# Bringing the slot weights to four groups of partitions with ScalarE copies in place of TensorE products

## The chip, the cores and the metric

The kernel runs on one core of one Trainium2 chip. The metric is the device time of one execution in microseconds (us); smaller is better. Three runs of the kernel before gave 720.49, 721.75 and 723.82 us, with a median of 721.75 us. Five engines work side by side, each in its own order and tied to the others by semaphores: TensorE (PE, with its weight loads as PEld), VectorE (DVE), ScalarE (ACT), GpSimd (POOL) and SyncE (SP), which issues the transfers.

## The reference, cut to what matters

The program is three layers, one behind the other, over 8 batches of 576 rows (4608 rows in all, 512 columns): a Nystrom attention, a gated feed-forward layer with 1536 hidden columns, and a soft mixture of 8 experts with 4 slots each, 32 slots in all. The change lies in the third:

```
logits = x @ phi                     # 4608 x 32
d = exp(logits - logits.max(0)); d /= d.sum(0)      # softmax down the rows, for each slot
slot_input = d.T @ x                 # 32 x 512
for e in range(8):                   # four slots for each expert
    slot_out[4*e:4*e+4] = relu(slot_input[4*e:4*e+4] @ w1[e]) @ w2[e]
c = exp(logits - logits.max(1)); c /= c.sum(1)      # softmax over the slots, for each row
out = c @ slot_out
```

The kernel never forms x. It keeps the hidden values h of the feed-forward layer (x = h @ w_out), sums `d.T @ h` batch by batch with a running maximum, and multiplies by w_out once at the end.

## The kernel before, in words

A batch is 48 places in the program: 12 blocks j of 128 hidden columns, with two halves of 288 rows each, with a gate product and a value product in each half. `unit` does one block. For each half `mm3` writes the gate product into a PSUM bank (`pg`, six matmuls), ScalarE makes `u` out of it (in the trace L299, the helper that records it, or L887, a tanh, in three of the 24 halves of batches 1 to 6, where DVE then finishes `u` at L888), `mm3` writes the value product into `pv`, and DVE multiplies the two into `hT` (L900 or L902). `logits` adds the block's share of the logits (`l`, L759), and `transposes` puts the hidden values into `HB` with rows on partitions (L764). The weights of the next two blocks come from `g_product` (`g`, L707) as a high part `GH` (ScalarE, L730) and a low part `GL` (DVE, L744).

All other work is laid between these places by tables (`SCHED`): the attention of the batch after, its row softmax, and, for the batch before, `softmoe`. A line of the table lists the places at which a generator runs on to its next `yield`; for `softmoe` that is `'sm': [1, 3, 5, 10, 17, 19, 20, 23, 24, 24, 27]`, so the step that the change touches is called at place 20 and the products that need it at place 23 of the batch that follows. The last batch has no batch behind it: its `softmoe` runs by itself after the last block, with `keep_warm` products (`warm`) between its steps. The Tile framework then places the instructions of each engine in an order of its own and sets the semaphores.

What `softmoe` does around the change: ScalarE raises the logits `LT` to their exponentials; DVE transposes them into `DN` (L820), 32 rows on each of the four groups of 32 partitions, `[128, 5 blocks, 32 slots]`. The sum over the rows of a batch is made of 32x32 tiles of TensorE: 18 row blocks times four column groups a, accumulated in four PSUM banks `m_d` (L844, 72 matmuls, shown as 144 in the trace since each is run in two parts). A tile reads its weights from its own group of 32 partitions, and row block g of `DN` lies on group g alone. So before the products every group of partitions must hold the weights of every row block. In the kernel before, `msum` (the 32x32 unit matrix repeated) times group g of `DN` gives a copy of that group on all 128 partitions: four products `m_dr` (L830), and four copies out of PSUM into `DR`, two by DVE and two by ScalarE (L833). `DR` lies in a spare part of the other batch's `HB`, so the trace calls it HB.

`m_dr`, `m_d` (three of its four banks), `g` and the attention's `m_a` and `m_c` all take turns in three PSUM banks with the tag `x`; the fourth bank of `m_d` is one of the two `pv` banks. After the products DVE adds them to the running sum `Sacc` (L852).

After the last batch come the products of the sum with w_out (`m_si`, L1107), the experts (`m_f`, L1153 and L1201), and the output (`m_o`, L1184). Their weights w1 and w2 are loaded ahead into buffers that come free on the way (`ffn_prefetch`, L962, and L970 in the end part).

Of the kernel before, what the change touches and what calls it, by code (L numbers as in the profile page):

```python
# [8 lines left out]
F32 = mybir.dt.float32  # L9
# [46 lines left out]
def nystrom_softmoe_kernel(  # L56
# [15 lines left out]
    pe, act, dve, pool, sp = nc.tensor, nc.scalar, nc.vector, nc.gpsimd, nc.sync  # L72
# [11 lines left out]
    psp = ctx.enter_context(tc.tile_pool(name="psp", bufs=1, space=PSUM))  # L84
# [7 lines left out]
    msum = cst[:, 256:384]  # L92
# [13 lines left out]
    DN = cp.tile([128, 5, M], F32, name="DN")  # L106
# [13 lines left out]
    spare = [HB[i][:, 6144:6912] for i in range(2)]  # L120
# [172 lines left out]
    def in_order(kind, *a, **kw):  # L293
        other = fence.get("exp" if kind == "silu" else "silu")
        if other is None:
            i = act.activation(*a, **kw)
        else:
            with tc.issue_after(other):
                i = act.activation(*a, **kw)  # L299
        fence[kind] = getattr(i, "ins", i)  # L300
# [467 lines left out]
    def keep_warm(n):  # L768

        m = psp.tile([128, 512], F32, tag="l", name="warm")  # L770
        for _ in range(n):
            pe.matmul(m[:, 0:160], ident, cst[:, 128:288], start=True, stop=True)
# [3 lines left out]
    def softmoe(b):  # L776
        L = L_t[b]
        assert ("l", b, NJ - 1) in seq
        act.copy(LT[:, 0:128], L[:, 0:128])
        act.copy(LT[0:64, 128:160], L[0:64, 128:160])  # L780

        pool.memset(LT[64:128, 128:160], -3e38)
        yield
        cm = smp.tile([128, 1], F32, tag="cm", name="cm")
        dve.tensor_reduce(cm, LT, axis=AX.X, op=ALU.max)
        c = CN[:, b]
        dve.transpose(c, LT.rearrange("p (k r) -> p k r", r=32))
        yield
        m = psp.tile([128, 512], F32, tag="x", name="m_x", bufs=3)
        pe.transpose(m[0:1, 0:128], cm[:, 0:1], ident)  # L790
        if b == nb - 1:
            keep_warm(WARM[0])
        row = smp.tile([1, 4, M], F32, tag="row", name="row")
        gm = smp.tile([1, M], F32, tag="gm", name="gm") if b else gmax
        dve.tensor_reduce(gm, m[0:1, 0:128].rearrange("p (c s) -> p s c", c=4), axis=AX.X, op=ALU.max)
        if b:
            dve.tensor_tensor(out=gmax, in0=gm, in1=gmax, op=ALU.max)
        dve.tensor_scalar(row, gmax.unsqueeze(1).to_broadcast([1, 4, M]), -1.0, None, ALU.mult)
        yield
        m = psp.tile([128, 512], F32, tag="x", name="m_y", bufs=3)  # L800
        pe.matmul(m[:, 0:1], row.rearrange("p c s -> p (c s)"), one, start=True, stop=True)
        mb = smp.tile([128, 2], F32, tag="mb", name="mb", bufs=2)
        dve.tensor_copy(mb[:, 0:1], m[:, 0:1])
        if b:
            dve.tensor_tensor(out=mb[:, 1:2], in0=mb[:, 0:1], in1=mb_t[-1][:, 0:1], op=ALU.subtract)
        mb_t.append(mb)
        mx = smp.tile([128, 5], F32, tag="mxc", name="mxc")
        bc = mx.unsqueeze(2).to_broadcast([128, 5, M])
        dve.tensor_reduce(mx, c, axis=AX.X, op=ALU.max)
        dve.tensor_tensor(out=c, in0=c, in1=bc, op=ALU.subtract)  # L810
        yield
        in_order("exp", LT, LT, AF.Exp, bias=mb[:, 0:1], accum_out=dsum)
        if b == nb - 1:
            keep_warm(WARM[1])
        al = smp.tile([128, 1], F32, tag="al", name="al")
        if b:
            in_order("exp", al, mb[:, 1:2], AF.Exp)
        in_order("exp", c, c, AF.Exp)
        yield
        dve.transpose(DN, LT.rearrange("p (k r) -> p k r", r=32))  # L820
        if b:
            dve.scalar_tensor_tensor(out=den, in0=den, scalar=al, in1=dsum, op0=ALU.mult, op1=ALU.add)
        else:
            dve.tensor_copy(den, dsum)
        yield

        DR = spare[(b + 1) % 2][:, 0:640].rearrange("p (g k s) -> p g k s", g=4, k=5)
        for g in range(4):
            m = psp.tile([128, 512], F32, tag="x", name="m_dr", bufs=3)
            pe.matmul(m[:, 0:160], msum[32 * g:32 * g + 32, :], DN[32 * g:32 * g + 32].rearrange("p k s -> p (k s)"),  # L830
                      start=True, stop=True)
            o = DR[:, g].rearrange("p k s -> p (k s)")
            act.copy(o, m[:, 0:160]) if g % 2 else dve.tensor_copy(o, m[:, 0:160])  # L833
        if b == nb - 1:
            keep_warm(WARM[2])
        yield

        assert ("h", b, NJ - 1) in seq
        ms = [psp.tile([128, 512], F32, tag="x" if a < 3 else "pv", name="m_d", bufs=3 if a < 3 else 2) for a in range(4)]
        hb = HB[b % 2].rearrange("p (j t f) -> p j t f", j=NJ, f=32)  # L840
        for k in range(5):
            for g in range(4 if k < 4 else 2):
                for a in range(4):
                    pe.matmul(ms[a][32 * g:32 * g + 32, 0:384].rearrange("p (j f) -> p j f", j=NJ),  # L844
                              DR[32 * a:32 * a + 32, g, k, :], hb[32 * a:32 * a + 32, :, 4 * k + g, :],
                              start=k == 0, stop=k == (4 if g < 2 else 3))
        if b == nb - 1:
            keep_warm(WARM[3])
        yield
        for a in (3, 0, 1, 2):  # L850
            if b:
                i = dve.scalar_tensor_tensor(out=Sacc[:, a], in0=Sacc[:, a], scalar=al, in1=ms[a][:, 0:384],  # L852
                                             op0=ALU.mult, op1=ALU.add)
                fence["sum"] = getattr(i, "ins", i)
            else:
                act.copy(Sacc[:, a], ms[a][:, 0:384])
            if a == 0:
                yield
        yield
        dve.tensor_reduce(mx, c, axis=AX.X, op=ALU.add)  # L860
        dve.tensor_scalar(mx, mx, 1e-9, None, ALU.add)
        dve.reciprocal(mx, mx)
        dve.tensor_tensor(out=c, in0=c, in1=bc, op=ALU.mult)
        yield
# [55 lines left out]
    for x in S_["loads"]:  # L920
        k, n = x[0], x[1:]
# [94 lines left out]
    for a in range(1, nb):  # L1016
        att, asm = attention(a), a_softmax(a)
        for gen, nm in ((att, "at"), (asm, "am")):
            for r in S_[nm + str(min(a, 3))]:
                todo[48 * (a - 1) + r].append(gen)  # L1020
        sm = softmoe(a - 1)
        for r in S_["sm"]:
            todo[48 * a + r].append(sm)
    prev = None
    for b in range(nb):
        for j in range(NJ):
            p = prev
# [40 lines left out]
    for _ in softmoe(nb - 1):  # L1068
        pass
# [11 lines left out]
    m = psp.tile([128, 512], F32, tag="x", name="m_s", bufs=3)  # L1081

    for a in (3, 0, 1, 2):
        for i in range(3):
            pe.matmul(m[:, 128 * i + 32 * a:128 * i + 32 * a + 32], Sacc[:, a, 128 * i:128 * i + 128], i4,
                      start=True, stop=True)
# [16 lines left out]
    m = psp.tile([128, 512], F32, tag="x", name="m_si", bufs=3)  # L1103
    for j in range(NJ):
        i, fb = divmod(j, 4)
# [5 lines left out]
    m = psp.tile([128, 512], F32, tag="x", name="m_sit", bufs=3)  # L1111
# [3 lines left out]
    for g in range(2):  # L1115
        for z, c in ((ZP3, slice(0, 3)), (ZP1, slice(3, 4))):
            for i in range(c.stop - c.start):
                o = z[:, i, 4 * g:4 * g + 4, 0:24].rearrange("p j (a x) -> p j a x", a=3)[:, :, :, 4 * g:4 * g + 4]
# [28 lines left out]
    for nh in range(2):  # L1147
        m = psp.tile([128, 512], F32, tag="pg", name="m_f1", bufs=2)
        for g in range(2):
            for c in range(4):  # L1150
                t = 8 * nh + 4 * g + c
                for e in range(4):
                    pe.matmul(m[32 * e:32 * e + 32, :], ZP[c][:, 4 * g + e, :], ffn_t[t][e],  # L1153
                              start=(g, c) == (0, 0), stop=(g, c) == (1, 3))
                pump(t + 1 + NT)
        act.activation(hF, m, AF.Relu)
        m = psp.tile([128, 512], F32, tag="x", name="m_ft", bufs=3)
        for i in range(4):
            pe.transpose(m[:, 128 * i:128 * i + 128], hF[:, 128 * i:128 * i + 128], ident)
        for g in range(2):  # L1160
            o = FT[:, g, 4 * nh:4 * nh + 4, :].rearrange("p i (x h s) -> p (i x) h s", h=2, s=4)[:, :, g, :]
# [32 lines left out]
    for dh in range(2):  # L1194
        m = psp.tile([128, 512], F32, tag="pg", name="m_f2", bufs=2)
# [72 lines left out]
```

## Time and profile before

| | |
|---|---|
| median of 3 runs | 721.75 us (720.49 to 723.82) |
| the profiled execution | 720.9 us, its span 719.1 us |
| TensorE matmul busy | 661.3 us (92%) |
| DVE busy | 510.8 us (71%) |
| ScalarE busy | 315.5 us (44%) |
| moved by the DMA queues | 105.04 MB, mean 146 GB/s |
| mean granted TensorE clock | 0.964 of full speed |

A busy share is a mean over the span. Where two engines take turns within a batch, a share says little about which of them ends last at a given place; that is read from the timeline and from the chain of work that ended last. Starts in the rows are us from the start of the span. In a row of the timeline, the number after the start is the time from the first start to the last end of the instructions that the row merges (`x2`, `x144`); what stands in brackets is the time for which the engine stood idle before it and the instruction that ended it.

### The profile page before, as it was taken

How to read it: one execution, taken by the hardware profiler on the slowest of the kernel's cores; microseconds unless marked ns; L12 is line 12 of the kernel's file. 1: busy time of each engine (PE TensorE's matmuls, PEld its weight loads, DVE VectorE, ACT ScalarE, POOL GpSimd, SP SyncE). 2: the span in 40 equal slices, each digit the busy share in tenths (PEclk: the TensorE clock that was granted, in tenths of full speed). 3: DMA queues.
4: the chain of work that ended last, by engine and by line, in shares of the span. 5: the costliest groups of instructions: out<-in, count | busy, mean ns of one | idle time of the engine just before them, and what ended most of it. 6: DMA issues, size and time to landing. Idle time of an engine off the chain costs nothing.

```text
span 719.1 us, 18723 instructions
## 1 busy us (share of the span) xinstructions
PE 661.3 (92%) x7755; PEld 488.0 (68%) x7755; DVE 510.8 (71%) x1222; ACT 315.5 (44%) x803; POOL 115.7 (16%) x132
## 2 busy tenths in 40 slices
PE   5787888999999999999999999999999999999980
PEld 2664566777687778767776877687778777773550
DVE  5999999877865896689578957885796664530441
ACT  2566766535533643264327333733363342311430
POOL 0544464401200120021012001200120000010000
PEclk9797898999999999999999999999999999999996
DMA  8687645304220431034012402240211399669999
GB/s 292 224 299 277 236 168 196 132 18 133 68 67 2 132 97 39 8 126 134 1 54 82 134 1 67 68 133 1 67 61 61 111 316 275 203 216 308 348 367 320
DMA packets 59989, 105.04 MB, mean 146 GB/s; under 512 B 3968, under 2 KB 29696, under 8 KB 58368
## 3 DMA queue, kind: packets, MB, share of 16 engines
q1 hardware_dynamic: 59904, 103.84, 44.1%
q8 instruction: 61, 1.00, 0.6%
q14 instruction: 24, 0.20, 0.1%
HBM read 91.24 MB, written 12.58 MB: 144 GB/s over the span
## 4 chain that ended last, share of the span: by engine, by line
PE 67%; DVE 17%; DMA 5%; ACT 5%; issue 3%; POOL 2%; SPq 0%; DVEq 0%; POOLq 0%; ACTq 0%
PE pg L873 20%; PE pv L873 17%; PE g L707 6%; PE l L759 5%; PE m_d L844 4%; PE m_n L634 3%; PE m_f L1153 2%; PE m_a L526 2%; DMA out_dram<-ob 1%; DVE w L179 1%; DMA HB<-in_w_dram 1%; DVE bd L309 1%; PE m_c L526 1%; DMA ffn<-in_w_dram 1%; DVE HB L179 1%
## 5 line engine op out<-in xcount | busy, mean ns | idle before, releaser
L299 ACT ACTIVATE u<-pg 128x288 f32<-128x288 f32 x174 | 71.5, 411 | 153.0 <-PE pg L873 146.3
L902 DVE TENSOR_TENSOR hT<-u,pv 128x288 f32<-128x288 f32 x162 | 72.9, 450 | 54.4 <-PE pv L873 47.6
L873 PE MATMUL pg<-EH,GH 128*128 128x288 f32 x384 | 98.2, 333 | 3.2 <-ACT GH L730 2.4
L873 PE MATMUL pv<-EH,GH 128*128 128x288 f32 x384 | 92.3, 314 | 0.8 <-DVE hT L902 0.8
L873 PE MATMUL pg<-EH,GL 128*128 128x288 f32 x384 | 87.1, 302 | 0.2 <-DVE GL L744 0.2
L744 DVE TENSOR_TENSOR GL<-g,GH 128x512 fp32r<-128x512 f32 (+1 forms) x114 | 63.2, 579 | 32.8 <-ACT GH L730 32.0
L873 PE MATMUL pg<-EL,GH 128*128 128x288 f32 x384 | 84.8, 302 | 0.0
L873 PE MATMUL pv<-EH,GL 128*128 128x288 f32 x384 | 84.6, 298 | 0.0
L873 PE MATMUL pv<-EL,GH 128*128 128x288 f32 x384 | 83.7, 299 | 0.0
L873 PEld LDWEIGHTS pg<-EH,GH 128*128 128x128 f32 x384 | 61.1, 192 | 25.0 <-issue 18.8
L764 DVE STREAM_TRANSPOSE HB<-hT 128x576 f32<-128x576 f32 x96 | 73.9, 770 | 1.6 <-POOL hT L898 0.2
L873 PEld LDWEIGHTS pv<-EH,GH 128*128 128x128 f32 x384 | 62.1, 190 | 18.4 <-issue 16.8
L730 ACT CAST GH<-g 128x512 fp32r<-128x512 f32 (+1 forms) x114 | 51.6, 505 | 51.0 <-PE g L707 50.8
L873 PEld LDWEIGHTS pg<-EH,GL 128*128 128x128 f32 x384 | 63.5, 191 | 2.5 <-issue 1.5
L873 PEld LDWEIGHTS pg<-EL,GH 128*128 128x128 f32 x384 | 62.6, 192 | 3.4 <-issue 3.4
L873 PEld LDWEIGHTS pv<-EH,GL 128*128 128x128 f32 x384 | 63.3, 191 | 0.0
L873 PEld LDWEIGHTS pv<-EL,GH 128*128 128x128 f32 x384 | 62.7, 191 | 0.0
L707 PE MATMUL g<-w,WB 64*32 64x512 f32 (+1 forms) x976 | 59.3, 511 | 1.6 <-DVE nx L621 0.7
L759 PE MATMUL l<-hT,P_sb 128*32 128x128 f32 (+1 forms) x768 | 48.5, 301 | 0.6 <-DVE hT L902 0.6
L759 PEld LDWEIGHTS l<-hT,P_sb 128*32 128x32 f32 x768 | 16.2, 109 | 40.0 <-issue 18.0
L680 POOL TENSOR_TENSOR AN<-AN,mxA 128x576 f32<-128x576 f32 x16 | 18.3, 1165 | 152.8 <-DVE mxA L679 136.9
L844 PE MATMUL m_d<-HB,HB 32*32 32x384 f32 x1152 | 40.7, 491 | 0.3 <-DVE GL L744 0.3
(252 smaller groups left out, 1057.5 us busy)
## 6 DMA issues: line engine op xcount, KB each, us to landing
k<-in_kT_dram SPq DMA_DIRECT2D x52, 288.0 KB, 3.9
ffn<-in_w_dram SPq DMA_DIRECT2D x13, 1024.0 KB, 9.2
ffn<-in_w_dram SPq DMA_DIRECT2D x24, 512.0 KB, 8.8
HB<-in_w_cat_dram SPq DMA_DIRECT2D x8, 1024.0 KB, 6.5
v<-in_v_dram SPq DMA_DIRECT2D x8, 1024.0 KB, 5.8
q<-in_qT_dram SPq DMA_DIRECT2D x28, 288.0 KB, 3.5
HB<-in_w_out_dram SPq DMA_DIRECT2D x12, 512.0 KB, 5.4
out_dram<-ob SPq DMA_DIRECT2D x5, 1024.0 KB, 10.4
```

The source lines that it names most:

```text
L299: i = act.activation(*a, **kw)
L526: pe.matmul(ms[r][32 * hp:32 * hp + 32, 0:HALF], lm[64 * r:64 * r + 64, hp, :], qk_t[nm, b, hp][64 * r:64 * r + 64, HALF * half:HALF * hal ...
L634: pe.matmul(m[:, 96 * q:96 * q + 96], bd[:, q, :], RV[:, q, :], start=True, stop=True)
L680: lambda q: pool.tensor_tensor(out=AN[q], in0=AN[q], in1=bc[q], op=ALU.subtract),
L707: pe.matmul(gs[r][32 * hp:32 * hp + 32, 0:256 * n].rearrange("p (u f) -> p u f", u=n), WB[b % 2][64 * r:64 * r + 64, hp, :], w[64 * r:64 * ...
L730: act.copy(H_, g)
L744: dve.tensor_tensor(out=GL, in0=g, in1=GH, op=ALU.subtract)
L759: pe.matmul(L[32 * c:32 * c + 32, 0:32 * k], P_sb[:, j, :], main[:, 0:k, c, :], start=j == 0, stop=j == NJ - 1)
L764: dve.transpose(HB[b % 2][:, S * j:S * j + S].rearrange("p (t r) -> p t r", r=32), hT[:, 0:S].rearrange("p (t r) -> p t r", r=32))
L844: pe.matmul(ms[a][32 * g:32 * g + 32, 0:384].rearrange("p (j f) -> p j f", j=NJ), DR[32 * a:32 * a + 32, g, k, :], hb[32 * a:32 * a + 32, ...
L873: pe.matmul(ps[:, 0:HALF], G_t[b, j, q, sel_][h], e[:, q, ts_], start=n == 0, stop=n == 5)
L902: dve.tensor_tensor(out=o, in0=u, in1=pv[:, 0:HALF], op=ALU.mult)
```

## The change

The four products and their four copies go. Group a of partitions needs row block g; with `DX[a ^ g]` in place of `DR[:, g]`, block g is read by group a from the tile of number a XOR g. `DX[0]` is `DN` itself. `DX[1]` is `DN` with groups 0 and 1 and groups 2 and 3 exchanged (four copies of 32 partitions), `DX[2]` is `DN` with the two halves of 64 partitions exchanged (two copies), and `DX[3]` is `DX[1]` with its halves exchanged (two copies, which must wait for `DX[1]`). All eight copies are 160 elements long on 32 or 64 partitions, read SBUF and write SBUF at other partitions, and are ScalarE's; in the last batch three of them are DVE's. The products `m_d` keep their number, shapes and order.

```diff
-        DR = spare[(b + 1) % 2][:, 0:640].rearrange("p (g k s) -> p g k s", g=4, k=5)
-        for g in range(4):
-            m = psp.tile([128, 512], F32, tag="x", name="m_dr", bufs=3)
-            pe.matmul(m[:, 0:160], msum[32 * g:32 * g + 32, :], DN[32 * g:32 * g + 32].rearrange("p k s -> p (k s)"),
-                      start=True, stop=True)
-            o = DR[:, g].rearrange("p k s -> p (k s)")
-            act.copy(o, m[:, 0:160]) if g % 2 else dve.tensor_copy(o, m[:, 0:160])
+
+        DX = [DN] + [spare[(b + 1) % 2][:, 160 * i:160 * i + 160].rearrange("p (k s) -> p k s", k=5) for i in range(3)]
+        for i, (x, src, to, fro, n) in enumerate(((2, 0, 0, 64, 64), (1, 0, 0, 32, 32), (1, 0, 32, 0, 32), (2, 0, 64, 0, 64),
+                                                  (1, 0, 64, 96, 32), (1, 0, 96, 64, 32), (3, 1, 0, 64, 64), (3, 1, 64, 0, 64))):
+            if b == nb - 1 and i in (0, 3, 7):
+                dve.tensor_copy(DX[x][to:to + n], DX[src][fro:fro + n])
+            else:
+                act.copy(DX[x][to:to + n], DX[src][fro:fro + n])
...
-                              DR[32 * a:32 * a + 32, g, k, :], hb[32 * a:32 * a + 32, :, 4 * k + g, :],
+                              DX[a ^ g][32 * a:32 * a + 32, k, :], hb[32 * a:32 * a + 32, :, 4 * k + g, :],
```

Where this stands on the engines: the orders below are those of ScalarE and TensorE in the blocks 4 and 5 of batch 3, where the weights of batch 2 are brought out, and of ScalarE after the last block. A line number of the changed kernel is larger by one from L830 on (L887 is L888 there, and so on).

ScalarE in batch 3, before: `CE` are the attention's scores, `u` the gate halves, `GH` the weights of the next two blocks.

```order
L557 COPY CE_3745<-m_c 128x320
L557 COPY CE_3746<-m_c 128x320
L887 ACTIVATE u<-pg 128x288
L833 COPY HB_86<-m_dr 128x160 x2
L299 ACTIVATE CE_3745,stat<-CE_3745,stat 128x576
L299 ACTIVATE CE_3745,stat<-CE_3745,stat 128x32
L299 ACTIVATE CE_3746,stat<-CE_3746,stat 128x576
L730 CAST GH<-g 128x512 x2
```

The same place in the changed kernel:

```order
L557 COPY CE_3737<-m_c 128x320
L557 COPY CE_3738<-m_c 128x320
L834 COPY HB_86<-DN 64x160
L834 COPY HB_86<-DN 32x160 x2
L834 COPY HB_86<-DN 64x160
L888 ACTIVATE u<-pg 128x288
L834 COPY HB_86<-DN 32x160 x2
L834 COPY HB_86<-HB_86 64x160 x2
L299 ACTIVATE CE_3737,stat<-CE_3737,stat 128x576
L299 ACTIVATE CE_3737,stat<-CE_3737,stat 128x32
L299 ACTIVATE CE_3738,stat<-CE_3738,stat 128x576
L730 CAST GH<-g 128x512 x2
```

Four copies now stand ahead of `u` and four behind it, in place of two behind it; the exponentials and `GH` keep their order behind them. Of the pair that reads HB, the first waits for ScalarE's own copies.

TensorE at the same place, before: two value products are parted by the last of the four `m_dr`.

```order
L873 MATMUL pg<-EH,GL 128x288 x2
L830 MATMUL m_dr<-DN,cst 128x160 x3
L873 MATMUL pv<-EH,GH 128x288
L830 MATMUL m_dr<-DN,cst 128x160
L873 MATMUL pv<-EH,GH 128x288
L873 MATMUL pv<-EL,GH 128x288 x2
L873 MATMUL pv<-EH,GL 128x288 x2
L707 MATMUL g<-w_602,WB_76 32x512 x8
```

In the changed kernel the four `m_dr` are gone and all else stands as it did, `m_d` too, one block later. On DVE the two copies L833 are gone, between L571 and L568 in batch 3, and nothing else moved.

ScalarE after the last block, before:

```order
L299 ACT_TABLE_LOAD
L299 ACTIVATE CN<-CN 128x160
L299 ACTIVATE LT,dsum<-LT,mb 128x160
L299 ACTIVATE al<-mb 128x1
L833 COPY HB_85<-m_dr 128x160 x2
L1133 CAST HB_86<-CN 128x20x8
```

And in the changed kernel:

```order
L299 ACT_TABLE_LOAD
L299 ACTIVATE CN<-CN 128x160
L299 ACTIVATE LT,dsum<-LT,mb 128x160
L299 ACTIVATE al<-mb 128x1
L834 COPY HB_85<-DN 32x160 x4
L834 COPY HB_85<-HB_85 64x160
L1134 CAST HB_86<-CN 128x20x8
```

Here ScalarE makes `DX[1]` and half of `DX[3]`; DVE makes `DX[2]` right behind `DN`, and, behind a reciprocal and a product (L862 and L863 of the kernel before), the other half of `DX[3]`. On TensorE the four `m_dr` between `warm` and `m_d` are gone.

## Rows read from the trace of the kernel before

**Rows 1.** The page's part 4: shares of the chain that ended last, by engine.

```profile
PE 67%; DVE 17%; DMA 5%; ACT 5%; issue 3%; POOL 2%; SPq 0%; DVEq 0%; POOLq 0%; ACTq 0%
```

**Rows 2.** Instructions on m_dr: count, ns min/median/max, first and last start, forms.

```profile
L830 PE MATMUL m_dr<-DN,cst x64: 294/346/399, 175.4 to 634.3; 32*128 32x160 f32 x64
```

**Rows 3.** The chain that ended last, in batch 3: start us, us, what.

```profile
317.78 0.53 DVE HB L833 x2
...
320.95 1.29 DVE GL L744 x2
```

**Rows 4.** Timeline of batch 3, 311.5 to 328 us: start, us, engine, instruction.

```profile
313.40 0.33 ACT L299 ACTIVATE CN<-CN 128x160 f32<-128x160 f32 x1
...
313.62 0.68 ACT L299 ACTIVATE AN<-AN 128x576 f32<-128x576 f32 x1
...
315.06 0.76 ACT L557 COPY CE<-m_c 128x320 f32<-128x320 f32 x2
...
315.62 0.43 PE L873 MATMUL pg<-EH,GL 128*128 128x288 f32 x2
...
316.09 0.41 ACT L887 ACTIVATE u<-pg 128x288 f32<-128x288 f32 x1 [0.27 <-PE pg L873]
...
317.28 0.45 DVE L888 SCALAR_TENSOR_TENSOR u<-u,pg 128x288 f32<-128x288 f32 x1
...
317.88 0.78 ACT L299 ACTIVATE CE<-CE,stat 128x576 f32<-128x576 f32 x1
...
318.26 1.09 PE L707 MATMUL g<-w,WB 64*32 64x512 f32 x16
...
319.58 0.78 ACT L299 ACTIVATE CE<-CE,stat 128x576 f32<-128x576 f32 x1 [0.53 <-DVE stat L571]
...
320.30 0.43 PE L873 MATMUL pg<-EH,GL 128*128 128x288 f32 x2
...
320.36 1.05 ACT L730 CAST GH<-g 128x512 fp32r<-128x512 f32 x2
...
321.45 5.14 PE L844 MATMUL m_d<-HB,HB 32*32 32x384 f32 x144
...
322.29 0.46 PEld L844 LDWEIGHTS m_d<-HB,HB 32*32 32x32 f32 x33 [0.46 <-DVE GL L744]
```

**Rows 5.** Timeline of batch 7, 586 to 602 us.

```profile
589.82 0.43 PE L873 MATMUL pg<-EH,GL 128*128 128x288 f32 x2
...
590.34 0.71 ACT L299 ACTIVATE u<-pg 128x288 f32<-128x288 f32 x2
...
592.61 0.66 PE L707 MATMUL g<-w,WB 64*32 64x256 f32 x16
...
593.36 0.65 ACT L730 CAST GH<-g 128x256 fp32r<-128x256 f32 x2 [1.21 <-PE g L707]
...
593.76 0.76 DVE L744 TENSOR_TENSOR GL<-g,GH 128x256 fp32r<-128x256 f32 x2 [0.53 <-ACT GH L730]
...
595.38 4.32 PE L844 MATMUL m_d<-HB,HB 32*32 32x384 f32 x144
```

**Rows 6.** Timeline after the last block, 625 to 645 us.

```profile
630.63 2.55 PE L772 MATMUL warm<-cst 128*128 128x160 f32 x12
...
631.01 0.43 ACT L299 ACTIVATE LT<-LT,mb 128x160 f32<-128x160 f32 x1 [1.11 <-DVE mb L803]
...
631.57 0.35 DVE L820 STREAM_TRANSPOSE DN<-LT 128x160 f32<-128x160 f32 x1
...
634.98 3.59 PEld L844 LDWEIGHTS m_d<-HB,HB 32*32 32x32 f32 x140 [0.31 <-ACT HB L833]
```

**Rows 7.** SP's waits, 640 to 719 us: engine line waited for: total, times, longest.

```profile
SPq L970 <- PE m_si L1107: 5.7, 2, 5.4
```

**Rows 8.** Busy time by stretch: per engine, then clock, DMA share, GB/s.

```profile
644.00:648.00 4.00, 4.00 (x96) 3.54 (x88) 0.01 (x1) 0.00 (x0) 0.00 (x0) 0.64 0.25 65
652.00:656.00 4.00, 4.00 (x42) 1.15 (x33) 0.00 (x0) 0.00 (x0) 0.00 (x0) 1.00 1.03 344
```

## The prediction, made before the changed kernel ran

> **What bounds the kernel now.** I read the chain of work that ended last first, since the busy shares lie near each other and do not say who waits. TensorE holds 67% of that chain and DVE 17% [rows 1], so both have stretches of their own, and the question at each of the eight places of the change is which of the two is late there. Then I read the rows of the instructions that go, then the timeline at the three kinds of place: batch 3 for the six alike ones (the weights brought out in batches 1 to 6), batch 7, and the end behind the last block.
>
> In batch 3 the four products `m_dr` stand in TensorE's way: from the last gate pair ahead of them to `g` it takes 318.26 - 315.62 = 2.64 us. The same pairs without `m_dr` (gate pair, three value pairs, change to the next kind) take 321.45 - 320.30 = 1.15 us a little later [rows 4]. So `m_dr` costs TensorE 1.49 us there, although the instructions of a batch are only some 0.35 us each in the list and overlap [rows 2]. But TensorE is not the one that is late: at 322.29 `m_d` has stood for 0.46 us until the second `GL` ends, because two of its banks are those of `g` [rows 4]. `GL` waits for `GH`, `GH` stands on ScalarE behind the exponential at 319.58, and that one waited 0.53 us for DVE's L571. The chain runs accordingly through DVE in this stretch, and the two copies L833 are a link of it with 0.53 us [rows 3].
>
> In batch 7 there is no such wait: `GL` ends at 593.76 + 0.76 = 594.52, and `m_d` comes only at 595.38, when TensorE reaches it [rows 5]. Behind the last block nothing overlaps: `DN` is ready at 631.92, the warming products end at 633.18, and `m_d` runs freely only from 634.98, when the last copy out of PSUM is done [rows 6].
>
> **What a copy costs.** No row shows a ScalarE copy that moves data to other partitions. The nearest rows: the exponential of `CN`, 160 elements, SBUF to SBUF, lasts 0.33 us, and the next instruction starts 0.22 us after it (313.62 - 313.40) [rows 4]. This is the size and the memory of the new copies, so I take 0.22 us from start to start, and 0.33 us to the end where something waits for the result. The low end is no issue, since a cheaper copy could not gain more than the 0.53 us of DVE per batch. The high end is 0.43 us, the dearest ScalarE instruction of 160 elements [rows 6].
>
> **Batches 1 to 6.** Four copies start at 315.82, where the scores' copies end (315.06 + 0.76). `u` starts at 315.82 + 4 x 0.22 = 316.70 in place of 316.09. It is ready at 317.11, and DVE took it up only at 317.28, being busy until then: this delay is hidden, by 0.17 us. The slot of a `u` is 0.30 us (a pair lasts 0.71, one 0.41 [rows 4, 5]), so copies five and six start at 317.00 and 317.22. The seventh reads what ScalarE has just written and waits for the end of the sixth, 317.55. The eighth follows at 317.77, and the first exponential can start at 317.99, against 317.88 before. Before, ScalarE was free again 1.17 us after that start (319.58 - 0.53 - 317.88); now this is 319.16. DVE reaches L571 0.53 us sooner, so the second exponential may start at 319.05 by DVE and starts at 319.16 by ScalarE: 0.42 us sooner than 319.58. `GH`, `GL` and the free part of `m_d` follow by the same 0.42. `g` is ready long before (TensorE is 1.49 us ahead by then), and what TensorE gains beyond 0.42 turns into a longer wait of `m_d` for `GL`, about 0.46 + 1.49 - 0.42 = 1.5 us. Six batches: 6 x 0.42 = 2.5 us. Bounds: 6 x 0.53 = 3.2 us gained if ScalarE is never late; 7.6 us lost at 0.43 a copy (worked out under the rivals).
>
> **Batch 7.** TensorE from the gate pair to `g`: 592.61 - 589.82 = 2.79 us, against 1.15 without `m_dr`, so it would reach `m_d` 1.64 us sooner, at 593.74. ScalarE: the two `u` from 590.34 have their slots filled at 590.94; copies one to six from there, the sixth at 592.04, the seventh at its end, 592.37, the eighth 592.59, `GH` at 592.81 (before 593.36). `GL` follows 0.40 later and lasts 0.76 [rows 5], to 593.97. So `m_d` waits a little for `GL` and is free at 594.0: 1.4 us gained. Bounds: 1.64 if ScalarE is early enough, 0.3 lost at 0.43.
>
> **Behind the last block.** ScalarE's four copies start at 631.96, the fourth ends at 631.96 + 3 x 0.22 + 0.33 = 632.95. The two halves of `DX[3]` start then, one on each engine, and end by 633.28. The warming products end at 633.18 and cover all but 0.1 us of this. The fourth `m_d` already reads `DX[3]`, so the products run freely from 633.3 in place of 634.98: 1.65 us gained, 0.9 at 0.43 a copy, and not more than 1.8, since TensorE is at its warming products until 633.18.
>
> **Does it reach the end?** From 652 us the DMA engines are full with the experts' weights (share 1.03), so the gain counts only if that stream starts sooner. It does: at 644 to 648 us the share is 0.25 [rows 8], and SP stands 5.4 us at one load until the products `m_si` have freed its buffer [rows 7]. These come behind `m_d`, so the stream moves with TensorE.
>
> **The sum:** 2.5 + 1.4 + 1.65 = 5.5 us. The profiled execution took 720.9 us with a span of 719.1; 5.5 less is 715.4 us. The median of the runs lies 0.85 us above that execution, and the forecast is made against the median: 721.75 - 5.5 = 716.3 us. Its own range is 715 to 718: the bounds 3.2, 1.64 and 1.8 on the good side (6.6 us), and 1.8 us missing from the three terms on the other.
>
> **Rivals.**
>
> *Copies do not overlap.* Eight short copies one behind the other, each between other quarters of the partitions, may take their whole 0.33 us each. Batches 1 to 6: `u` ends at 315.82 + 1.32 + 0.41 = 317.55, 0.27 behind DVE's 317.28; the other four copies end at 318.87, ScalarE is free at 320.04, and the second exponential is 0.46 us late: 2.8 us lost. Batch 7: `GH` at 591.05 + 8 x 0.33 = 593.69, `GL` to 594.85, 0.5 us gained. The end: `DX[3]` at 631.96 + 1.32 + 0.33 = 633.61, 1.35 gained. In all 0.9 us lost, 722.7 us, which is no change. For it: no row has a copy across partitions. Against it: the row of `CN` shows the overlap at this size. [...]
>
> *Slower: ScalarE becomes the late engine.* The place is the stretch from the scores' copies to `GH` in batches 1 to 6, the price the length of a copy. At 0.43 us each `u` ends at 317.95, the copies at 319.67, ScalarE is free at 320.84 and `GH` 1.26 us late: 6 x 1.26 = 7.6 us lost. Batch 7: `GH` at 594.49, `GL` to 595.65, 0.3 lost. The end still gains 0.9. In all 7.0 us lost, 728.8 us. Between 0.33 and 0.43 a copy the sum grows by 6.1 us, so it is slower by over 0.5% (3.6 us) from 0.375 us a copy. For it: ScalarE has little idle time in that stretch (0.27 and 0.53 us in the rows) and eight copies take 1.8 us at best. Against: the 0.43 belongs to an instruction that also sums its output and takes a bias.
>
> *All of TensorE's time counts.* If `m_d` did not have to wait for `GL`, six times 1.49, with 1.64 and 1.65, would be 12.2 us: 709.5 us. The wait of 0.46 us that is there already speaks against it.
>
> *Nothing arrives.* If the stream of weights at the end started by something other than TensorE, all gains would be taken up there: 721.8 us. Rows 7 and 8 speak against it.
>
> **Chances.** Forecast 0.60, no overlap 0.22, ScalarE late 0.08, all of TensorE's time 0.05, nothing arrives 0.05. About 0.5% (3.6 us) is what a measurement of this kernel can tell from no change. Faster takes the forecast but for a small part that may fall short, and the fourth case: 0.62. Same takes the copies without overlap, the case in which nothing arrives, and that small part: 0.30. Slower is 0.08. For 8 in 10 the range must take in most of the second case, and at the low end some scatter of the runs (1.3 us from lowest to median) below 715: 713.5 to 723.0 us.
>
> **What the profile after would show.** ScalarE's copies with starts 0.22 us apart and the seventh behind the sixth's end; `u` ready before DVE asks for it; the second exponential of the scores no longer waiting for L571, or hardly; `m_d` in batches 1 to 6 waiting for `GL` some 1.5 us in place of 0.46, `GL` 0.4 us sooner by the batch's own clock; in batch 7 and at the end `m_d` 1.4 and 1.65 us sooner. Copies 0.33 us apart, or `GH` later than before against the start of the batch, would make the forecast wrong; so would a weight stream at the end that does not start sooner.

## The result, and the profile after

The changed kernel takes 725.11 us (median of 20 runs, 722.63 to 728.29) against 721.73 us before (20 runs, 716.88 to 725.35) beside it: ratio 1.0055 [1.004, 1.007], 4.0 us slower. The forecast was 716.3 us with a range of 713.5 to 723.0. The profiled execution took 722.93 us, its span is 721.1 us.

The page's part 4 of the changed kernel, shares of the chain that ended last, to be read against [rows 1]:

```profile
PE 69%; DVE 11%; ACT 11%; DMA 3%; issue 2%; POOL 1%; SPq 0%; DVEq 0%; POOLq 0%; ACTq 0%
```

DVE's 17% have become 11%, and ScalarE's 5% have become 11%: with the copies the chain runs less through DVE and more through ScalarE.

Batch 3 in the timeline of the changed kernel, to be read against [rows 4]:

```profile
313.81 0.43 ACT L299 ACTIVATE LT<-LT,mb 128x160 f32<-128x160 f32 x1
...
317.36 1.34 ACT L834 COPY HB<-DN 64x160 f32<-64x160 f32 x4
...
318.72 0.41 ACT L888 ACTIVATE u<-pg 128x288 f32<-128x288 f32 x1
319.16 0.65 ACT L834 COPY HB<-DN 32x160 f32<-32x160 f32 x2
319.17 0.46 DVE L889 SCALAR_TENSOR_TENSOR u<-u,pg 128x288 f32<-128x288 f32 x1 [0.29 <-ACT u L888]
...
319.84 0.67 ACT L834 COPY HB<-HB 64x160 f32<-64x160 f32 x2
...
320.53 0.78 ACT L299 ACTIVATE CE<-CE,stat 128x576 f32<-128x576 f32 x1
...
321.61 0.76 ACT L299 ACTIVATE CE<-CE,stat 128x576 f32<-128x576 f32 x1
...
321.81 0.83 PE L845 MATMUL m_d<-HB,DN 32*32 32x384 f32 x2
...
322.37 1.04 ACT L730 CAST GH<-g 128x512 fp32r<-128x512 f32 x2
322.97 1.29 DVE L744 TENSOR_TENSOR GL<-g,GH 128x512 fp32r<-128x512 f32 x2 [0.73 <-ACT GH L730]
...
323.71 0.13 PEld L845 LDWEIGHTS m_d<-HB,HB 32*32 32x32 f32 x2 [1.77 <-DVE GL L744]
...
324.31 0.11 PEld L845 LDWEIGHTS m_d<-HB,HB 32*32 32x32 f32 x3 [0.46 <-DVE GL L744]
```

Four copies take 1.34 us: (1.34 - 0.32) / 3 = 0.34 us from start to start, not 0.22. DVE waits 0.29 us for `u`, the second exponential waits for nothing but ScalarE, and `GH` follows it. The copies begin at nearly the same place of the batch as forecast, 3.55 us behind its first exponential (317.36 - 313.81; the forecast's 315.82 is 3.52 behind). The batches are compared from that exponential, at 313.81 us here. In the kernel before it is at 312.30, and at 587.65 in batch 7:

```profile
312.30 0.43 ACT L299 ACTIVATE LT<-LT,mb 128x160 f32<-128x160 f32 x1
...
587.65 0.43 ACT L299 ACTIVATE LT<-LT,mb 128x160 f32<-128x160 f32 x1
```

`GH` starts 8.56 us behind it, against 320.36 - 312.30 = 8.06: 0.50 us later, where 0.42 sooner was forecast. `m_d` runs freely after 10.50 us, against 9.99. Up to `GH` the chain through this stretch consists of ScalarE alone: eight copies with `u` between them, 1.94 us of exponentials, `GH`; then come `GL` and `m_d`.

More is lost behind that. Stretches of 2 us in the changed kernel (busy time of TensorE, its weight loads, DVE, ScalarE, GpSimd; then the granted clock, DMA share, GB/s):

```profile
322.00:324.00 2.00, 0.93 (x3) 0.13 (x2) 1.27 (x4) 2.00 (x7) 2.00 (x2) 1.00 0.00 0
324.00:326.00 2.00, 2.00 (x57) 1.10 (x65) 2.00 (x7) 0.62 (x3) 0.26 (x1) 0.73 0.00 0
326.00:328.00 2.00, 2.00 (x65) 1.08 (x35) 2.00 (x4) 1.98 (x7) 1.84 (x2) 0.50 0.03 8
328.00:330.00 2.00, 2.00 (x60) 1.17 (x42) 1.87 (x5) 0.65 (x1) 0.99 (x1) 0.92 0.00 0
```

In the kernel before, from the start of `m_d` in batch 3 to its end:

```profile
321.00:323.00 2.00, 2.00 (x41) 0.93 (x41) 2.00 (x5) 1.02 (x4) 1.83 (x2) 1.00 0.00 0
323.00:325.00 2.00, 2.00 (x93) 1.43 (x83) 2.00 (x5) 1.44 (x6) 0.68 (x1) 1.00 0.03 8
325.00:327.00 2.00, 2.00 (x49) 1.15 (x40) 2.00 (x3) 1.78 (x2) 2.00 (x2) 1.00 0.00 0
```

In the stretch of 2 us in which `m_d` of the changed kernel waits for `GL`, TensorE is busy for 0.93 us. Then the granted clock falls from 1.00 to 0.50 while `m_d` runs, and comes back before it is over. In the kernel before it is 1.00 through the same products. It falls in five of the six batches; the one left out, the fifth, shows the price: from its first exponential to the next batch's are 70.00 us, in batches 2 to 4 they are 71.16, 71.10 and 71.18. The kernel before has 69.83, 69.39 and 69.60 in those three, and 69.71 in the fifth. Within the batch, `m_d` ends 14.8 us behind the first exponential in the fifth and 16.2 to 16.3 us behind it in batches 2 to 4 and 6, though it runs freely after 10.5 us in all of them.

Batch 7 of the changed kernel, to be read against [rows 5]:

```profile
594.71 0.43 ACT L299 ACTIVATE LT<-LT,mb 128x160 f32<-128x160 f32 x1
...
598.14 2.01 ACT L834 COPY HB<-DN 64x160 f32<-64x160 f32 x6
...
600.75 0.63 ACT L730 CAST GH<-g 128x256 fp32r<-128x256 f32 x2
...
601.95 0.11 PEld L845 LDWEIGHTS m_d<-HB,HB 32*32 32x32 f32 x3 [0.20 <-DVE GL L744]
```

`m_d` is free 7.24 us behind the exponential, against 595.38 - 587.65 = 7.73: 0.49 us gained where 1.4 was forecast. Behind the last block, to be read against [rows 6]:

```profile
636.61 0.43 ACT L299 ACTIVATE LT<-LT,mb 128x160 f32<-128x160 f32 x1 [1.03 <-DVE mb L803]
...
637.54 1.34 ACT L834 COPY HB<-DN 32x160 f32<-32x160 f32 x4 [0.32 <-DVE DN L820]
637.62 0.49 DVE L832 COPY HB<-DN 64x160 f32<-64x160 f32 x2
...
639.01 0.11 PEld L845 LDWEIGHTS m_d<-HB,HB 32*32 32x32 f32 x2 [0.16 <-DVE HB L832]
```

`m_d` is free 2.40 us behind the exponential, against 634.98 - 631.01 = 3.97: 1.57 us gained, 1.65 forecast. DVE's two copies take 0.49 us, 0.25 apart; ScalarE's four are again 0.34 apart. `m_d` runs from when DVE's half of `DX[3]` is there; that half reads only two of ScalarE's four copies, so it need not wait for the fourth. What comes behind starts sooner by nearly as much: the products `m_s` stand 644.21 - 636.61 = 7.60 us behind the exponential, against 640.05 - 631.01 = 9.04 before (that kernel's row), and SP's longest wait for `m_si` is 4.7 us where [rows 7] has 5.4.

```profile
640.05 2.87 PE L1085 MATMUL m_s<-cst,Sacc 128*128 128x32 f32 x24
```

In the changed kernel, in the timeline and among SP's waits:

```profile
644.21 2.87 PE L1086 MATMUL m_s<-cst,Sacc 128*128 128x32 f32 x24 [0.19 <-DVE Sacc L853]
```

```profile
SPq L971 <- PE m_si L1108: 4.7, 1, 4.7
```

### The profile page after: what moved, and what is told of

It reads as the page before. It is cut to its first block, busy times and chain, and to the rows that moved or that the text cites. A ratio compares the mean times of both kernels' runs of the same rounds, so it can differ in the third digit from the quotient of the medians.

```text
span 721.1 us, 18610 instructions
## 1 busy us (share of the span) xinstructions
PE 654.6 (91%) x7691; PEld 481.9 (67%) x7691; DVE 508.2 (70%) x1209; ACT 329.7 (46%) x848; POOL 114.3 (16%) x132
## 4 chain that ended last, share of the span: by engine, by line
PE 69%; DVE 11%; ACT 11%; DMA 3%; issue 2%; POOL 1%; SPq 0%; DVEq 0%; POOLq 0%; ACTq 0%
PE pg L874 20%; PE pv L874 17%; PE m_d L845 6%; PE g L707 6%; PE l L759 5%; PE m_n L634 3%; PE m_f L1154 2%; ACT HB L834 2%; DVE w L179 2%; ACT CE L299 2%; PE m_a L526 2%; DMA out_dram<-ob 1%; PE m_v L615 1%; ACT L299 1%; DMA HB<-in_w_dram 1%
## 5 line engine op out<-in xcount | busy, mean ns | idle before, releaser
L874 PE MATMUL pv<-EH,GH 128*128 128x288 f32 x384 | 89.5, 310 | 0.3 <-DVE hT L903 0.3
L845 PE MATMUL m_d<-HB,HB 32*32 32x384 f32 x864 | 46.7, 599 | 8.6 <-DVE GL L744 8.6
L845 PE MATMUL m_d<-HB,DN 32*32 32x384 f32 x288 | 46.0, 596 | 0.0
L845 PEld LDWEIGHTS m_d<-HB,HB 32*32 32x32 f32 x864 | 24.7, 114 | 27.7 <-DVE GL L744 16.7
```

What stands on the lines that cost most here:

```text
L874: pe.matmul(ps[:, 0:HALF], G_t[b, j, q, sel_][h], e[:, q, ts_], start=n == 0, stop=n == 5)
```

## The experiments

All ratios are against the kernel before, run beside each kernel. "A batch" is the time from its first exponential to the next one's, in one profiled execution.

**Products kept for TensorE's sake (a test that decides nothing).** In batches 1 to 6 the four products of before were added to the copies, and nobody read their result.

```
+        if b < nb - 2:
+            for g in range(4):
+                m = psp.tile([128, 512], F32, tag="x", name="m_dr", bufs=3)
+                pe.matmul(m[:, 0:160], msum[32 * g:32 * g + 32, :], DN[32 * g:32 * g + 32]..., start=True, stop=True)
```

> The changed kernel with the four products m_dr put back in batches 1 to 6, their results read by nobody; the copies stay ScalarE's. Theory A (TensorE's clock): in the changed kernel m_d waits 1.4 us for GL with TensorE idle, the granted clock then stands at 0.50 for some 4 us, and m_d takes 7.2 us with its waits instead of 5.7. The extra 1.5 us of products lie in that wait, so the clock stays at 1.00, each of the six batches becomes 1.2 to 1.7 us shorter than in the changed kernel (70.0 us as the one undisturbed batch, against 71.1 to 71.7), and the time is about 718 us, 0.990 of the changed kernel's and 0.995 of the kernel's before. Theory B (the copies are ScalarE's lateness alone): nothing in the wait for GL changes, the time is the changed kernel's, about 725 us. Theory C (m_d itself is slower with weights from DN and three tiles): same as B, with m_d still at 7.2 us.

Measured: 731.10 us, ratio 1.0154 [1.0124, 1.0184]. No theory is told apart by it, since the edit also moved other work: one exponential more stands ahead of `GH` on ScalarE now, `GL` comes later still, `m_d` waits for it as before (1.6 to 1.8 us, then 0.9, in batches 2 to 6), and the clock still falls under `m_d` in three of the six batches, and once elsewhere in the first. A filler has to leave the other engines' order alone; the sixth experiment does.

**Copies in batch 7 and at the end alone**, products in batches 1 to 6 (`by_copy = b >= nb - 2`), run twice:

> Copies only for the last two batches' weights (batch 7 and behind the last block); products and their copies as before in batches 1 to 6. All theories put the loss into batches 1 to 6 and a gain into the rest: batch 7 1.4 to 1.5 us and the end 1.65 us by the working of the prediction, up to 3.6 us by the two profiles: 716.7 to 718.6 us, a ratio of 0.993 to 0.996. If the end's 3.6 us were only the scatter of one run, the ratio stays above 0.995.

> Once more the kernel with copies in the last two batches alone, beside the one with copies in the first six alone, on one chip: what the last two batches gain. By the profiles (one execution each) seven kernels with copies in the last two batches took 84.4 to 85.8 us from the last softmax to the end, two with products 87.3 and 88.1; with the last step that would be 3 to 4 us of gain, ratio 0.995 against the kernel before. By the first timing of this kernel (0.9988) it is 0.9 us, ratio 0.998 to 1.000.

Measured: 719.83 us, 0.9988 [0.9968, 1.0009], and 719.46 us, 0.9972 [0.995, 0.9993]. The middle of the two, 0.998, is 1.4 us gained; the intervals reach from about no gain to 2.3 and 3.6 us. No clock falls in the first six batches of either. In both profiles this kernel loses some time inside the last `m_d` that the changed kernel doesn't lose; in the first of them:

```profile
635.64 0.11 PEld L855 LDWEIGHTS m_d<-HB,HB 32*32 32x32 f32 x2 [1.09 <-issue]
```

The weight loads stand for 1.09 us (0.83 in the second) and wait for no other engine. The traces also hold the packets of the queue q8, whose kind the page gives as "instruction" (61 packets, 1.00 MB in the kernel before), and one of them landed 1.4 us (1.3 in the second) before the loads went on. The same holds for all 12 idle times of TensorE of over 0.3 us marked "issue" that the fourteen traces have from 150 us on: a packet of q8 landed 1.3 to 1.7 us before each ended (in the kernel before 1.45 us ahead of the end, at 603.68, of an idle time of 0.79 us). That a late packet is the cause is my reading and not shown: no run here moves it. The 2.1 us that the changed kernel gains at these two places in its rows (0.49 and 1.57) lie inside both intervals. My expectation of 3 to 4 us from single profiles was too much: the time from the last exponential to the end differs by 2.5 us between the two profiles of this one kernel (85.6 and 88.1 us). The clock has a part in that: in the second the granted clock is 0.71 from 640 to 644 us and 0.50 from 644 to 648, in the first 1.00. The kernel before has such a fall there too (0.64 in [rows 8]) and the changed kernel's profile has none, so the end of one execution can't be held against that of another for less than these 2.5 us.

**Copies in batches 1 to 6 alone** (`by_copy = b < nb - 2`), also run twice:

> Copies only in batches 1 to 6, the end as before. Theory A: six batches with the lengths of the changed kernel's profile, 7.9 us more in all: about 729 us, a ratio of 1.011. Theory B, with copies that do not overlap but no loss of clock: 6 x 0.46 = 2.8 us more, 724.5 us, 1.004.

> Once more the kernel with copies in the first six batches alone. Theory CLOCK: what the changed kernel loses, and the gain of the last two batches besides: ratio 1.007 if that gain is 0.9 us, 1.011 if it is 4 us.

Measured: 728.51 us, 1.0122 [1.0088, 1.0155], and 728.95 us, 1.0095 [1.0065, 1.0124], some 7 to 9 us lost. Theory A's 1.011 is met, and theory B's 1.004 lies outside both intervals; the second expectation's 1.007 and 1.011 can't be told apart. So the loss comes from the six alike batches. With the 1.4 us gained elsewhere the two parts come to 6 us lost, 2 us more than the whole change loses; why they don't add up is not shown. The clock falls in five of the six batches in the first profile and in four in the second, which holds both cases in one execution. Batches 2 and 3 in stretches of 4 us (columns as above):

```profile
252.00:256.00 4.00, 2.61 (x41) 0.99 (x40) 3.27 (x11) 3.07 (x11) 2.27 (x2) 1.00 0.00 1
256.00:260.00 4.00, 4.00 (x127) 2.56 (x111) 4.00 (x7) 3.22 (x7) 2.80 (x2) 1.00 0.03 8
324.00:328.00 4.00, 3.29 (x84) 1.89 (x99) 4.00 (x9) 2.61 (x10) 2.11 (x3) 0.79 0.00 0
328.00:332.00 4.00, 4.00 (x82) 2.85 (x59) 3.77 (x9) 1.63 (x2) 1.99 (x2) 0.78 0.02 4
```

`m_d` waits 2.1 and 0.5 us for `GL` in both, the clock falls in batch 3 alone, and batch 2 takes 69.96 us, batch 3 71.22. Batches 4 and 5 repeat it with 69.69 (no fall) and 71.23 (fall). So one fall costs about 1.4 us. What decides whether it comes in a given batch isn't settled.

**Three copies of the whole tile in place of eight**, so that no copy changes its partitions:

```
-        for i, (x, src, to, fro, n) in enumerate(((2, 0, 0, 64, 64), ...)):
-            ...
+        for i in range(1, 4):
+            act.copy(DX[i], DN)
```

> In place of the eight copies, three copies of the whole of DN, 128 partitions, to the three other tiles, without an exchange of partitions (so the weights of the row blocks are wrong, and the time alone counts). If copies fail to overlap because they start at other partitions, these stand 0.22 us apart; if any copy from SBUF to SBUF does so, 0.33. Either way ScalarE is 1.7 to 2 us less loaded: GH is 0.4 us sooner than in the kernel before, as DVE allows. Theory A: m_d still waits some 1.4 us for GL with TensorE idle, the clock still falls, and batches 1 to 6 are 0.5 to 1.2 us longer than before: total 0.999 to 1.004 of before. Theory B: they are 0.4 us shorter, and the total is 717 us or less, 0.992.

Measured: 714.45 us, 0.9928 [0.990, 0.9957]. Batch 3, its first exponential at 311.35:

```profile
314.74 0.81 ACT L830 COPY HB<-DN 128x160 f32<-128x160 f32 x3
...
318.94 1.05 ACT L730 CAST GH<-g 128x512 fp32r<-128x512 f32 x2
```

Three copies of 0.36 us in 0.81 us, 0.23 apart; `GH` 7.59 us behind the exponential, 0.47 sooner than before; `m_d` waits 1.1 and 0.5 us for `GL` in batches 2 to 6, and the clock falls in the first batch alone. Theory B holds. With copies that overlap, the forecast's chain of reasoning comes out (5.2 us gained, where 5.5 were forecast), though with three copies ScalarE also has less to do than with the forecast's eight.

**The copy by itself**, one form in each batch:

```
+        FORMS = ([(1 + i % 3, 0, 0, 0, 64) for i in range(8)],
+                 [(1 + i // 2 % 3, 0, 64 * (i % 2), 64 * (i % 2), 64) for i in range(8)], ...)
-        for i, (x, src, to, fro, n) in enumerate(((2, 0, 0, 64, 64), ...)):
+        for i, (x, src, to, fro, n) in enumerate(FORMS[b] if b < nb - 2 else own):
```

> A measurement of the copy by itself: the eight ScalarE copies of each of the first six batches take another form in each batch (so the slot weights of those batches are not the right ones). Batch 1: 64 partitions from 0 to 0, eight times. Batch 2: 64 partitions in place, alternately at 0 and at 64. Batch 3: from 64 to 0, eight times. Batch 4: alternately 64 to 0 and 0 to 64. Batch 5: 32 partitions in place at 0, 32, 64, 96. Batch 6: all 128 partitions in place. Theory START (a copy overlaps the one before only if it starts at the same partitions): 0.22 to 0.25 us apart in batches 1, 3 and 6, 0.33 in 2, 4 and 5. Theory SHIFT (what stops the overlap is that source and target lie at different partitions): 0.22 to 0.25 in batches 1, 2, 5 and 6, 0.33 in 3 and 4. Theory SIZE (copies of fewer than 128 partitions do not overlap): 0.33 in batches 1 to 5, 0.24 in batch 6.

> A second measurement of the copy by itself, again with one form of ScalarE's eight copies in each of the first six batches (so the slot weights of the first five are not the right ones). Batch 1: 64 partitions, target always 0, source alternately 0 and 64. Batch 2: source always 0, target alternately 0 and 64. Batch 3: from 0 to 0, 64 and 32 partitions in turn. Batch 4: 32 partitions in place, always at 32. Batch 5: 64 partitions in place, always at 64. Batch 6: the eight copies of the changed kernel itself, in an order that puts those with one target start behind each other as far as their dependences let them. Theory SOURCE (the start of what is read decides): 0.22 to 0.25 us apart in batch 2, 0.33 in batch 1. Theory TARGET (the start of what is written decides): the reverse. Theory BOTH (a change of either stops the overlap): 0.33 in both. All three: 0.22 to 0.25 in batches 3 to 5; batch 6 is shorter than the changed kernel's eight only by TARGET, then by some 0.3 us.

Each kernel was run once; what counts are the distances within it. The first kernel, one line each of batches 1 to 6 in this order:

```profile
174.97 1.02 ACT L841 COPY HB<-DN 64x160 f32<-64x160 f32 x4
...
245.79 1.36 ACT L841 COPY HB<-DN 64x160 f32<-64x160 f32 x4
...
315.87 1.00 ACT L841 COPY HB<-DN 64x160 f32<-64x160 f32 x4
...
385.04 1.36 ACT L841 COPY HB<-DN 64x160 f32<-64x160 f32 x4
...
454.79 1.32 ACT L841 COPY HB<-DN 32x160 f32<-32x160 f32 x4
...
525.76 1.03 ACT L841 COPY HB<-DN 128x160 f32<-128x160 f32 x4
```

Four copies take 1.00 to 1.03 us where start and target stay the same from copy to copy, also from 64 to 0, and 1.32 to 1.36 where they change, also in place. Each lasts 0.32 (64 and 32 partitions) to 0.36 us (128), so they are 0.22 to 0.23 apart in the one case and 0.33 to 0.36 in the other. Theory START holds; SHIFT and SIZE fall. The second kernel, batches 2, 4, 5 and 6:

```profile
246.49 1.38 ACT L842 COPY HB<-DN 64x160 f32<-64x160 f32 x4
...
386.57 1.00 ACT L842 COPY HB<-DN 32x160 f32<-32x160 f32 x4
...
455.67 1.00 ACT L842 COPY HB<-DN 64x160 f32<-64x160 f32 x4
...
525.17 1.35 ACT L842 COPY HB<-DN 32x160 f32<-32x160 f32 x4
```

A change of target alone stops the overlap (1.38), so SOURCE falls. 32 partitions at 32 or 64 at 64 overlap as well as any, and so do 64 and 32 partitions in turn (batch 3, 0.21 to 0.23 apart). Batch 6, the real eight copies sorted by target start, gains nothing: where neighbours there have one target they read from different starts, and the copies are 0.33 to 0.36 apart. In batch 1 (source alternates) the copies have five distances with nothing between them; four are 0.32 to 0.36 and one is 0.23. Between which two that is I couldn't make out: in batch 3 the trace shows that the copies do not run in the program's order (64, 64, 32, 32 partitions where the program has 64 and 32 in turn). So BOTH is likely, and TARGET alone is spoken against by batch 6. Of the eight copies only two pairs agree in both starts, (0 from 64) twice and (64 from 0) twice; an order that puts each pair together, worth some 2 x 0.11 us a batch, wasn't tried.

**TensorE's wait filled, and nothing else.** Five products into `m_d`'s first bank, which `m_d` then overwrites; ScalarE, DVE, GpSimd and SP keep their order.

```
+        if b < nb - 2:
+            for _ in range(5):
+                pe.matmul(ms[0][:, 0:160], ident, cst[:, 128:288], start=True, stop=True)
         for k in range(5):
```

> As the changed kernel, with five products of 128 weight columns and 160 moved columns on TensorE just ahead of the m_d products of the first six batches; their result is written into m_d's first bank and overwritten, so nothing but TensorE's idle time changes (the order on ScalarE, VectorE and GpSimd stays as it was). Theory CLOCK (the copies make GH and GL late by some 1 us; TensorE then stands idle for about 1.5 us inside m_d, and the granted clock falls to 0.50 for the products that follow, in five of six batches): the clock stays at 1.00 in m_d, a batch takes about 70.0 us in place of 71.2, and the kernel takes about 719 us, ratio 0.995 to 1.000 against the kernel before. Theory LATE (only the delay of GH and GL counts, the clock's fall is a by-product): the batches stay at 71.1 us or grow by what the five products put off, 725 to 727 us, ratio 1.005 to 1.008.

Measured: 720.27 us, 0.9992 [0.997, 1.0015]. Batch 3, its first exponential at 311.90 (x10: the profile counts each of the five twice), and the clock:

```profile
319.48 1.52 PE L844 MATMUL m_d<-cst 128*128 128x160 f32 x10
320.46 1.04 ACT L730 CAST GH<-g 128x512 fp32r<-128x512 f32 x2
...
322.40 0.12 PEld L848 LDWEIGHTS m_d<-HB,HB 32*32 32x32 f32 x3 [0.47 <-DVE GL L744]
```

```profile
320.00:322.00 2.00, 1.95 (x11) 1.02 (x10) 1.27 (x4) 2.00 (x7) 1.92 (x2) 1.00 0.00 0
322.00:324.00 2.00, 2.00 (x68) 1.02 (x68) 2.00 (x7) 0.62 (x2) 0.35 (x1) 1.00 0.00 0
324.00:326.00 2.00, 2.00 (x90) 1.46 (x74) 2.00 (x4) 1.98 (x7) 1.74 (x2) 1.00 0.03 8
```

`GH` stands 8.56 us behind the exponential and `m_d` is free after 10.50 us, both as late as in the changed kernel. Only the clock differs: 1.00 in all six `m_d`, and batches 2 to 5 take 69.7 to 70.2 us. In batches 2 to 6 `m_d` ends 14.8 us behind the exponential, as in the one batch of the changed kernel without a fall. Theory CLOCK holds, LATE falls. From its free start to its end `m_d` takes 4.29 us in batch 3, as in the kernel before, so the products are not slower with weights from several tiles, and theory C of the first experiment falls too. Adding useless products makes the kernel (1.0055 - 0.9992) x 721.7 = 4.5 us faster, 2.6 to 6.4 with the two intervals combined as independent ones.

**The copies on GpSimd** in the first six batches, then with the filler, then in batch 7 too:

```
-                act.copy(DX[x][to:to + n], DX[src][fro:fro + n])
+                (act.copy if b >= nb - 2 else pool.tensor_copy)(DX[x][to:to + n], DX[src][fro:fro + n])
```

> As the changed kernel, but in the first six batches the eight copies are made by GpSimd in place of ScalarE; the last two batches keep them on ScalarE and VectorE. Theory CLOCK: ScalarE loses 2.7 us of work a batch, GH starts some 0.5 us sooner than in the changed kernel (322.37), TensorE's wait inside m_d shortens to about 1 us, the clock mostly keeps 1.00, and the kernel takes 714 to 718 us, ratio 0.990 to 0.996. Rival: GpSimd's copies (not in the trace; a 128x576 product takes it 1.13 us, so some 0.35 to 0.45 us each by columns, eight of them 3 to 3.6 us after DN at 314.85) end too late or hold up VectorE beside them: m_d waits for them or for GL as long as before, the clock falls, 722 to 726 us.

> The GpSimd copies and the five filling products on TensorE together. Theory CLOCK: clock 1.00 in all six m_d, 714 to 717 us, ratio 0.990 to 0.995, no slower than with GpSimd's copies alone. Rival (the filling products only put m_d off, since GL is there sooner): 1 to 3 us more than with GpSimd's copies alone.

> As the kernel with GpSimd's copies in the first six batches, with GpSimd's copies in the seventh as well (the last keeps ScalarE and VectorE). In the seventh batch the copies stand on ScalarE ahead of GH there, and m_d waits 0.9 us for GH and GL. If that wait goes with the copies, 0.5 to 1.2 us less than with GpSimd in six batches: ratio 0.992 to 0.995. If the copies themselves end later on GpSimd (0.36 us apart against 0.33), no change, 0.995; with a fall of the clock in the seventh m_d 1 to 2 us more.

Measured: 717.78 us, 0.9947 [0.9921, 0.9974]; with the filler 717.42 us, 0.9947 [0.9921, 0.9973]; in seven batches 716.27 us, 0.9938 [0.9914, 0.9961]. The first of them in batch 3, its first exponential at 311.13:

```profile
312.16 2.19 POOL L834 COPY HB<-DN 64x160 f32<-64x160 f32 x6 [4.71 <-DVE DN L820]
...
316.84 0.78 ACT L299 ACTIVATE CE<-CE,stat 128x576 f32<-128x576 f32 x1 [1.50 <-DVE stat L571]
...
318.85 1.05 ACT L730 CAST GH<-g 128x512 fp32r<-128x512 f32 x2
```

GpSimd was idle there and has all eight copies done by 315.10 (the last two start at 314.41 and take 0.69 us), 3.7 us ahead of `m_d`. ScalarE waits for DVE again, and `GH` comes 7.72 us behind the exponential: 0.84 sooner than in the changed kernel, 0.34 sooner than before. `m_d` waits 1.3 and 0.5 us in batches 2 to 6, and the clock stays at 1.00 in all six batches without any filler. So the filler has nothing to mend: theory CLOCK's figures for it came out (1.00, 0.990 to 0.995, no slower) without putting it to a test, and of the rival's 1 to 3 us lost nothing can be seen. The seventh batch's gain can't be told from none: in its profile `m_d` starts freely there after 6.09 us in place of 7.25, but then stands 2.2 us in a stall marked "issue". These versions beat both kernels.

## Why the prediction was wrong

- **The step that failed first is the price of a copy**, "0.22 us from start to start", taken from the exponential of `CN` and its neighbour. Those two, and every nearby row, use all 128 partitions and so start at the same one. The new copies change their start partitions from one to the next, and are 0.34 apart. The text named this as a rival with 22 chances in 100; the row that it held against it could not speak to it. With late copies, but the clock held at 1.00, 0.6 us are gained (0.9992 [0.997, 1.0015]) where 5.5 were forecast.
- **The rival's mechanism came out, place by place.** Batches 1 to 6: `GH` 0.50 us late (0.46 in the rival). Batch 7: 0.49 gained (0.5). The end: 1.57 gained (1.35). Its sum of 0.9 us lost, 722.7 us, is just inside the interval of the kernel whose clock doesn't fall (719.5 to 722.8 us). Not all of the 0.50 us reaches the next batch: the six batches of that kernel are 0.1 to 0.5 us longer than before, 0.3 in the mean of one execution each. The rival's price of 0.33 us a copy, the full length in the row of `CN`, agrees with the measured distance where the starts change (0.32 to 0.36), and not where they stay (0.21 to 0.23).
- **A term was put at nothing: the clock.** That `m_d` would wait some 1.5 us for `GL` was foreseen, as time that costs nothing. A wait of that size did come out nearly free: with three overlapping copies `m_d` waits 1.1 and 0.5 us, and the clock falls in one batch of six. With late copies it waits 1.8 and 0.5 us in batch 3 and 2.1 and 0.5 in batches 2 and 4 to 6, and the clock falls to 0.50 under the products behind it in five batches of six. With that wait filled the kernel is 4.5 us faster, so the clock costs as much as the whole change loses (4.0 us [2.9, 5.1]). These two numbers come from the same ratio 1.0055 and don't confirm each other; five falls at 1.1 to 1.5 us each would be 5.5 to 7.5 us, and the number of falls differs from execution to execution. The clock is also what carried the time out of the range, whose upper end was the rival with nothing beyond it.
- **Right was** the reading that DVE, not TensorE, was late in the six batches: with copies that overlap, or on an idle engine, `GH` comes 0.34 to 0.47 us sooner (0.42 forecast) and the kernel at 714 to 718 us. "Slower" at 728.8 us by copies of 0.43 us did not come; the copy is 0.32 us long.
- **The end's gain came out in size by luck** (1.57 for 1.65). ScalarE's fourth copy ends 2.27 us behind the exponential, where 632.95 - 631.01 = 1.94 was forecast; but `m_d` did not have to wait for it, since DVE's half of `DX[3]` reads two of the four copies.
- **The signs named beforehand** worked: copies 0.33 us apart and a `GH` later against the start of its batch were listed as what would make the forecast wrong, and both are in the first rows read.

## What to carry to other kernels

Price a new instruction by rows that change their start partitions as it will, as well as by its size; where all rows start at the same partition, they do not give the distance between instructions whose starts change. Here that was 0.32 to 0.36 us, against 0.21 to 0.23 with equal starts, and the full length (0.32 us) was the nearer value. Work taken from TensorE is not free where it was filling a wait: look what the granted clock does to the products behind a longer wait before calling that wait harmless (here 0.50 for 3.4 us in five batches of six, behind waits of 1.8 to 2.1 us). A helper operation belongs on the engine that the chain does not run through: here GpSimd, whose copies are as slow (0.37 us apart) but stand in nobody's way.

## What the runs showed of the hardware

- ScalarE copies of 160 elements, SBUF to SBUF, are 0.21 to 0.23 us apart when start and target partitions repeat (measured with 32, 64 and 128 partitions), and 0.32 to 0.36 when the target's start, or both starts, change (32 and 64 partitions). With the source's start alone changing, four distances of five were 0.32 to 0.36. It is the change that counts, not the distance between source and target.
- A 64-partition copy of 160 elements takes 0.32 us on ScalarE, 0.24 us on DVE (0.49 for two) and 0.32 us on GpSimd (0.37 apart, six in 2.19 us).
- A fall of TensorE's granted clock from 1.00 to 0.50 came after a stretch of 2 us with 0.93 us of TensorE work, lasted 3.4 us (by the stretches of batch 3: 1.1 of the first 2 us, the next 2 us, and 0.3 of the third) and cost a batch 1.1 to 1.5 us. In the same kernel some batches with a similar wait had none.
